# Softmax weights in PSUM, the mask on ScalarE, and two matmuls a bank in the last half chunk

## The chip, the cores and the metric

The kernel runs on one core of a Trainium2 chip. The metric is the device time of one execution in microseconds (us), the median of three runs: 639.03 us (638.97 to 640.16). Five engines work side by side, each with a queue of its own: TensorE (PE; its weight loads are listed as PEld), VectorE (DVE), ScalarE (ACT), GpSimd (POOL) and SyncE (SP), which here only issues DMAs. SBUF is the working memory; PSUM takes the results of matmuls. A PSUM bank is [128, 512] float32, and the core has eight.

## The reference, cut to what matters

```
x = A_x                                   # [2048, 640]
g = sigmoid((x * gate_w).sum(-1))
# A: 32 heads of 20, each position looks at 8 positions, 2 apart, at or before it
logits = einsum("bhsd,bhswd->bhsw", q, kg) * 20 ** -0.5
logits = where(idx >= 0, logits, -1e9)
a = einsum("bhsw,bhswd->bhsd", softmax(logits), vg) @ wo
# B: dense, Mish, dense, with 1728 hidden units
b = mish(x @ w1 + b1) @ w2
out = g * a + (1 - g) * b
```

## The kernel before, in words

All matmuls are float32 split in two: a high half, rounded to float32r, and a low half, the rest. `mm3` makes one product of three matmuls: high x high, high x low, low x high. For every operand ScalarE makes the high half (L337) and VectorE or GpSimd the low half (L340), into a `pair` tile. An operand thus costs one DMA, one ScalarE and one VectorE or GpSimd instruction before TensorE can use it.

The work in order of TensorE's stream: eight units of q, k, v (four groups of eight heads, two halves P of the positions), interleaved with the first layer (`mlp1`, 13 chunks of 128 hidden units by four blocks of 512 positions); then the second layer (`mlp2`); then the projection by wo (`wo_out`), whose VectorE sums (L954) form the output.

The second layer computes a 2 x 2 block product with seven products instead of eight, named a to g in `PRODUCTS`. Each has seven chunks of 128 hidden units (kc = 0 to 6). Its activations ("11", "21", "22", "t1" to "t4") lie in DRAM, written by `mish` with SP's DMAs and with GpSimd's adding DMAs (L613); its weights are w2 or sums of w2 (`s_d`, made by L704). 1728 = 13 x 128 + 64, so the last chunk of the second half of the hidden units has only 64 rows (FR); it meets kc = 6 of the products b, g and f. There the kernel before pads: the tiles keep 128 rows, the weights' lower 64 rows are zeros, the activations' lower rows are copies of finite data.

The attention runs on VectorE (`attention`), in two halves a unit: `scores` multiplies q by a window of k (L424) and sums over the head (L427) into `lg`; GpSimd adds -BIG/scale to the logits of partition 0 that look before the start (`bounded`, L435); VectorE takes the maximum (L442) and subtracts it (L443); ScalarE exponentiates (L444); `shares` divides by the sum, times the gate, and writes the weights `pw` (L452); `outputs` multiplies a window of v by `pw` (L458) and adds over the window (L463, L464, L466).

The order of every queue is written out by `Plan`: it walks through the tasks with a duration for each and hands out, engine by engine, what is ready, by rank. Low halves and a few sums may go to VectorE or GpSimd ("ANY"). While attention lasts, GpSimd may start such work only within a quiet time, and its instruction is then made to wait for the VectorE instruction ahead of that time (`follow`); quiet is, before, the sum L427 alone. Rings limit what is in flight: 8 banks, 21 pairs, 7 raw buffers.

Of the kernel before, what the change touches and what calls it, by code (L numbers as in the profile page):

```python
# [8 lines left out]
F32 = mybir.dt.float32  # L9
# [49 lines left out]
class Plan:  # L59
# [34 lines left out]
    def run(self):  # L94
# [34 lines left out]
        while left:  # L129
            again = not events or events[0][0] > now  # L130
            while again:
                again = False
                for e in self.LAG:
                    if busy[e]:
                        continue
                    fit = [t for t in ready[e] if fits(t)]
                    on = begun and loud
                    if e == "POOL":
                        fit += [t for t in shared if fits(t)]
                        if on:  # L140
                            fit = [t for t in fit if now + t.ns[0] <= quiet + 150 or t.rank < 0]
                    elif e == "DVE":
                        fit += [t for t in shared if fits(t) and (not on or due(t))]
                    if not fit:
                        continue
                    t = min(fit, key=lambda t: t.key)
                    if t.both:
                        shared.remove(t)
                        t.eng = e
                    else:  # L150
                        ready[e].remove(t)
                    if type(t.ns) is tuple:
                        t.ns = t.ns[e == "DVE"]
                    for b in t.take:
                        b.ring.free -= 1
                        b.ring.at += 1
                        b.t = b.make()
                    t.start = now
                    ins = t.fn(e) if t.both else t.fn()
                    if e == "POOL" and on and quiet > now and gate and ins:  # L160
                        self.follow(ins, gate)
                    if e == "DVE":
                        if t.kind:
                            begun = True
                            loud -= 1
                        if t.kind == "qk sum":
                            quiet, gate = now + t.ns, last
                        last = ins or last
                    if e == "PE":
                        begun_pe = max(begun_pe, t.pos)  # L170
                    busy[e] = again = True
                    end = over = now + t.ns * self.CARE.get(e, 1.0)
                    heapq.heappush(events, (over, n, "idle", e))
                    if t.land:
                        wire = max(wire, end) + t.land
                        end = wire + (0 if e == "SP" else self.ADDING)
# [36 lines left out]
def kernel(ctx: ExitStack, tc: tile.TileContext, x, wq, wo, w1, b1, w2, xt, gw, out):  # L213
# [3 lines left out]

    keep = ctx.enter_context(tc.tile_pool(name="keep", bufs=1))
    dram = ctx.enter_context(tc.tile_pool(name="dram", bufs=1, space=DRAM))
    psum = ctx.enter_context(tc.tile_pool(name="psum", bufs=8, space=PSUM))  # L220
    pe = ctx.enter_context(tc.tile_pool(name="pe", bufs=1, side="right"))
    at = ctx.enter_context(tc.tile_pool(name="at", bufs=1))

# [5 lines left out]
    plan = Plan({"bank": 8, "pair": NPAIR, "w": NW, "raw": NRAW, "raw1": 1, "hb": NH,  # L229
                 "ot": 1, "b": 11}, follow)  # L230

    def ps_buf():
        return plan.buf("bank", lambda: psum.tile([128, 512], F32, name="bank"))

    def pair_buf():
        return plan.buf("pair", lambda: pe.tile([128, 2, 512], F32R, name="pair", bufs=NPAIR))
# [31 lines left out]
    def mm_ns(n):  # L268
        return 13.5 + (n + 15) // 16 * 16 / 2.4
# [7 lines left out]

    A.preload_act_table_set("mish")
    bias = keep.tile([128, FC + 1], F32)
    bound = keep.tile([1, 7, 7], F32)  # L280
    zt = keep.tile([128, 2, 8], F32)
    gate = keep.tile([128, 2, 8], F32)
    gc = keep.tile([128, 2, 8], F32)
# [120 lines left out]
    def attention(u, P, hq, ready, gates):  # L404
# [27 lines left out]

        def bounded(a, b, after):
            b = min(b, 7)
            return add("POOL", 3400, lambda: G.tensor_tensor(lg[0:1, a:b, :, 0:7], lg[0:1, a:b, :, 0:7],  # L435
                       bound[:, a:b, None, :].to_broadcast([1, b - a, HQ, 7]), op=OP.add), [cg] + after, rank=-1)

        def softmax(a, rank, after):

# [176 lines left out]
    def mish(src, n, fc, tb, after, hold, late=0, home=None):  # L616
# [15 lines left out]
        def at(name):  # L632
            return name, P, kc

        def rest(name, of, after):

            return [put(at(name), of, after, rows=high)] if n < 128 else []

        if (half, h) == (0, 0):
            done[at("11")] = [put(at("11"), here, [a], [hb])]  # L640
            done[at("t1")] = [put(at("t1"), here, [a], [hb])]
        elif (half, h) == (0, 1):
            done[at("t3")] = [put(at("t3"), here, [a], [hb])]
            done[at("t1")] = [plus(at("t1"), here, [a] + done[at("t1")], [hb])]
        elif (half, h) == (1, 0):
            done[at("21")] = [put(at("21"), here, [a], [hb], low)]
            if n < 128:
                done[at("21")].append(dma(lambda: blk[at("21")][n:], here, [a], rank=0.5, hold=[hb], size=n * 2048))
            done[at("t4")] = [put(at("t4"), here, [a], [hb], low)] + rest("t4", lambda: blk[at("t1")][high], done[at("t1")])
        else:  # L650
            done[at("22")] = [put(at("22"), here, [a], [hb], low)]
            if n < 128:
                done[at("22")].append(dma(lambda: blk[at("22")][n:], here, [a], rank=0.5, hold=[hb], size=n * 2048))
            t2 = [put(at("t2"), here, [a], [hb], low)] + rest("t2", lambda: blk[at("t1")][high], done[at("t1")])
# [34 lines left out]
    def sums_of_w2(kc):  # L689
# [24 lines left out]
        s4 = sum_of((o2, 256), (o1, 256), (a2, 0), OP.subtract, [s3])  # L714
        m = add("ACT", act_ns(128), lambda: A.activation(apart.t[:, 256:384], apart.t[:, :128], AF.Copy, scale=-1.0), d[2:], rank=LATER, hold=[apart], late=2500)
        q = sum_of((apart, 384), (apart, 0), (apart, 128), OP.add, [m, s4], n=128)
        if kc == KH - 1:
            s4 = add("POOL", 300, lambda: G.memset(o2.t[FR:, 256:], 0.0), [s4], rank=-1.0, hold=[o2])
            q = add("POOL", 300, lambda: G.memset(apart.t[FR:, 384:], 0.0), [q], rank=-1.0, hold=[apart])
        done["s", kc] = [kept(0, 512, o1, 0, [s2]), kept(512, 256, o2, 0, [s3]), kept(896, 256, o2, 256, [s4]),  # L720
                         kept(768, 128, apart, 256, [m]), kept(1152, 128, apart, 384, [q])]

    def load_minus(src, n):

        raw, p = stage(True), pair_buf()
        d = dma(lambda: raw.t[:, :n], src, take=[raw], size=n * 512)
        a = add("ACT", act_ns(n), lambda: A.activation(p.t[:, 0, :n], raw.t[:, :n], AF.Copy, scale=-1.0), [d], rank=SOON, take=[p], hold=[raw])
        b = add("DVE", dve_ns(n), lambda: V.scalar_tensor_tensor(p.t[:, 1, :n], raw.t[:, :n], -1.0, p.t[:, 0, :n].bitcast(F32),
                op0=OP.mult, op1=OP.subtract), [a], rank=SOON, hold=[raw, p])
        p.ready = [a, b]  # L730
        return p

# [18 lines left out]
    def load_step(i):  # L751
        k, kc = steps[i]
        name, of, _ = PRODUCTS[k]
        at = 0
        if name == "a":
            p = load_pair(lambda: w2[kc][:, :384], "ANY", n=384, wide=i > 2)
        elif name == "b":
# [30 lines left out]
    def mlp2(mid):  # L788
# [72 lines left out]
        for i, (k, kc) in enumerate(steps):  # L861
# [17 lines left out]
            for part in parts:  # L879
# [7 lines left out]
                for c in kcs:  # L887
# [4 lines left out]
                    def run(part=part, keys=keys, p=p, at=at, acts=acts, first=first, stop=stop, names=names, name=name):  # L892
# [5 lines left out]
                    last = add("PE", 9 * len(part) / 3 * mm_ns(512), run,  # L898
                               [last] + p.ready + sum((acts[P].ready for P in Ps), []) + [read[key] for key in keys if key in read and c == 0],
                               take=take if c == kc else [], hold=[bank[key] for key in keys] + [p] + [acts[P] for P in Ps])  # L900
                    if c == KH - 1:
# [171 lines left out]
```

## Time and profile before

| what | value |
|---|---|
| median of three runs | 639.03 us |
| profiled execution: span, first to last instruction | 636.9 us (its time with start and end is not listed; the median lies 2.1 us above the span) |
| TensorE busy | 631.9 us, 99%, 2805 matmuls, granted clock 1.00 throughout |
| VectorE busy | 584.1 us, 92% |
| ScalarE, GpSimd busy | 277.4 us (44%), 215.2 us (34%) |
| a matmul with 512 columns | 386 ns long |
| chain that ended last | TensorE 99% |

How to read it: a row of a group names the line, engine, operation and tiles (out<-in), shapes, count, then busy us and the mean ns of one, then idle time in front of them. A timeline row has start, length, engine, line. Matmuls overlap, so the distance between two starts, not the length, is what one costs in a stream. An idle engine that nobody waits for costs nothing.

### The profile page before, as it was taken

How to read it: one execution, taken by the hardware profiler on the slowest of the kernel's cores; microseconds unless marked ns; L12 is line 12 of the kernel's file. 1: busy time of each engine (PE TensorE's matmuls, PEld its weight loads, DVE VectorE, ACT ScalarE, POOL GpSimd, SP SyncE). 2: the span in 40 equal slices, each digit the busy share in tenths (PEclk: the TensorE clock that was granted, in tenths of full speed). 3: DMA queues.
4: the chain of work that ended last, by engine and by line, in shares of the span. 5: the costliest groups of instructions: out<-in, count | busy, mean ns of one | idle time of the engine just before them, and what ended most of it. 6: DMA issues, size and time to landing. Idle time of an engine off the chain costs nothing.

```text
span 636.9 us, 8494 instructions
## 1 busy us (share of the span) xinstructions
PE 631.9 (99%) x2805; PEld 526.2 (83%) x2805; DVE 584.1 (92%) x584; ACT 277.4 (44%) x565; POOL 215.2 (34%) x157
## 2 busy tenths in 40 slices
PE   9999999999999999999999999999999999999997
PEld 6888888888888888888888888888888888888886
DVE  7888999999999999999899989799999999999941
ACT  7553353435436332542524244584676426721100
POOL 2212313131414442132343423204107328967310
PEclk9999999999999999999999999999999999999999
DMA  9999998867954994798499955989996758844642
GB/s 327 373 283 180 190 263 227 229 174 223 296 172 86 271 258 93 222 218 178 84 245 214 219 122 147 254 274 282 312 286 220 226 159 288 289 155 149 193 158 82
DMA packets 91323, 137.26 MB, mean 216 GB/s; under 512 B 12128, under 2 KB 41184, under 8 KB 91216
## 3 DMA queue, kind: packets, MB, share of 16 engines
q1 hardware_dynamic: 83600, 122.83, 62.6%
q0 software_dynamic: 7680, 13.90, 14.8%
q8 instruction: 22, 0.36, 0.2%
q14 instruction: 21, 0.17, 0.1%
HBM read 77.11 MB, written 57.81 MB: 212 GB/s over the span
## 4 chain that ended last, share of the span: by engine, by line
PE 99%; DVE 0%; issue 0%
PE bank L374 33%; PE bank L372 33%; PE bank L373 33%; PE bank L510 1%; PE bank L319 1%; DVE kvq L954 0%; DVE lg L315 0%
## 5 line engine op out<-in xcount | busy, mean ns | idle before, releaser
L372 PE MATMUL bank<-pair 128*128 128x512 f32 (+1 forms) x476 | 183.8, 386 | 0.0
L374 PE MATMUL bank<-pair 128*128 128x512 f32 (+1 forms) x476 | 183.7, 386 | 0.0
L373 PE MATMUL bank<-pair 128*128 128x512 f32 (+1 forms) x476 | 183.7, 386 | 0.0
L373 PEld LDWEIGHTS bank<-pair 128*128 128x128 f32 x476 | 89.3, 188 | 17.2
L374 PEld LDWEIGHTS bank<-pair 128*128 128x128 f32 x476 | 89.4, 188 | 17.1
L372 PEld LDWEIGHTS bank<-pair 128*128 128x128 f32 x476 | 89.3, 188 | 17.0
L424 DVE TENSOR_TENSOR pr<-kvq 128x2560 f32<-128x2560 f32 x32 | 90.8, 2839 | 3.5 <-DMA kvq<-kvq 1.6
L337 ACT ACTIVATE pair<-raw 128x512 fp32r<-128x512 f32 (+3 forms) x122 | 72.0, 615 | 48.4 <-DMA raw<-o 21.5
L458 DVE TENSOR_TENSOR pr<-kvq,pw 128x2560 f32<-128x2560 f32 x32 | 91.1, 2848 | 0.9
L427 DVE TENSOR_REDUCE lg<-pr 128x128 f32<-128x2560 f32 x32 | 90.2, 2818 | 0.6
L516 ACT ACTIVATE kvq<-bank 128x320 f32<-128x320 f32 x64 | 28.3, 442 | 114.7 <-PE bank L374 114.7
L435 POOL TENSOR_TENSOR lg<-lg,bound 1x168 f32<-1x168 f32 (+1 forms) x16 | 68.8, 4303 | 20.4 <-DVE lg L427 18.7
L625 ACT ACTIVATE hb<-bank,bias 128x512 f32<-128x512 f32 x52 | 35.9, 690 | 90.7 <-PE bank L374 77.2
L374 PE MATMUL bank<-pair,kvq 128*128 128x512 f32 (+1 forms) x188 | 72.6, 386 | 0.0
L372 PE MATMUL bank<-pair,kvq 128*128 128x512 f32 (+1 forms) x188 | 72.6, 386 | 0.0
L373 PE MATMUL bank<-pair,kvq 128*128 128x512 f32 (+1 forms) x188 | 72.6, 386 | 0.0
L340 POOL TENSOR_TENSOR pair<-raw,pair 128x496 fp32r<-128x496 f32 (+2 forms) x31 | 42.6, 1386 | 86.4 <-ACT pair L337 30.0
L372 PE MATMUL bank<-pair,w 128*128 128x512 f32 x182 | 70.8, 389 | 0.0
L373 PE MATMUL bank<-pair,w 128*128 128x512 f32 x182 | 70.8, 389 | 0.0
L374 PE MATMUL bank<-pair,w 128*128 128x512 f32 x182 | 70.8, 389 | 0.0
L340 DVE TENSOR_TENSOR pair<-raw,pair 128x512 fp32r<-128x512 f32 (+1 forms) x91 | 63.9, 721 | 5.2 <-ACT pair L337 5.2
L337 ACT ACTIVATE pair<-hb 128x512 fp32r<-128x512 f32 (+3 forms) x63 | 38.8, 615 | 42.7 <-DMA hb<-o 16.0
(89 smaller groups left out, 873.9 us busy)
## 6 DMA issues: line engine op xcount, KB each, us to landing
actt<-hb SPq DMA_DIRECT2D x52, 256.0 KB, 4.6
act<-hb SPq DMA_DIRECT2D x38, 256.0 KB, 4.6
raw<-actt SPq DMA_DIRECT2D x32, 256.0 KB, 4.5
raw<-act SPq DMA_DIRECT2D x29, 256.0 KB, 4.0
actt<-hb POOLq DMA_DIRECT2D x26, 256.0 KB, 6.2
actt<-actt POOLq DMA_DIRECT2D x24, 256.0 KB, 5.4
hb<-actt SPq DMA_DIRECT2D x24, 256.0 KB, 4.5
kvq<-in_xt SPq DMA_DIRECT2D x16, 320.0 KB, 7.2
```

The source lines that it names most:

```text
L319: nc.tensor.matmul(warm_bank.t, idle[:, :128], idle, start=True, stop=True)
L337: a = add("ACT", act_ns(n), lambda: A.activation(hi(), raw(), AF.Copy), after, rank=rank, take=take, hold=hold)
L340: return (V if e == "DVE" else G).tensor_tensor(lo(), raw(), hi().bitcast(F32), op=OP.subtract)
L372: nc.tensor.matmul(ps, ah, bh, start=first, stop=False, skip_group_check=more)
L373: nc.tensor.matmul(ps, ah, bl, start=False, stop=False, skip_group_check=more)
L374: nc.tensor.matmul(ps, al, bh, start=False, stop=last, skip_group_check=more)
L424: return V.tensor_tensor(pr, window(kv, s0, 0), q[:, s0:s0 + 2, None, :].to_broadcast([128, 2, W, QF]), op=OP.mult)
L427: V.tensor_reduce(lg_w[:, s0:s0 + 2], pr.rearrange("p s w (h d) -> p s w h d", d=DH), op=OP.add, axis=AX.X)
L435: return add("POOL", 3400, lambda: G.tensor_tensor(lg[0:1, a:b, :, 0:7], lg[0:1, a:b, :, 0:7], bound[:, a:b, None, :].to_broadcast([1, b - ...
L458: V.tensor_tensor(pr.rearrange("p s w (h d) -> p s w h d", d=DH), vw, pw[:, s0:s0 + 2, :, :, None].to_broadcast([128, 2, W, HQ, DH]), op=O ...
L516: a = add("ACT", 330, lambda: A.activation(kv[:, 7 + s], ps.t[:, QF:3 * QF].rearrange("p (a b) -> p a b", a=2), AF.Copy), [done] + before, ...
L625: a = add("ACT", 595, lambda: A.activation(to(it()), src(), AF.Mish, bias=bias[:n, fc:fc + 1]), after + [bias_in], rank=NEXT, take=[] if h ...
```

## The change

Three things change, and the planner's order follows.

The softmax weights `pw` move from SBUF to PSUM, into the eighth bank; matmuls keep seven. VectorE writes them there (L452) and reads them in L458, and the planner now counts that product, too, as a quiet time for GpSimd.

-BIG is no longer added by GpSimd. `bound` is filled with -BIG/scale, and ScalarE copies it over the logits, one small instruction for each of the seven positions concerned, 56 in all.

In the last chunk of b, g and f the 64 rows are loaded twice, into partitions 0 to 63 and 64 to 127. The weights' operand holds the high half above and the low half below, the activations' operand the high half in both; one matmul of 128 rows makes high x high + low x high, and one of 64 rows makes high x low. The padding DMAs and fills go.

```
-                        if t.kind == "qk sum":
+                        if t.kind in ("qk sum", "pv"):
                             quiet, gate = now + t.ns, last
...
-    psum = ctx.enter_context(tc.tile_pool(name="psum", bufs=8, space=PSUM))
+    NBANK = 7
+    psum = ctx.enter_context(tc.tile_pool(name="psum", bufs=1, space=PSUM))
...
-    pw = at.tile([128, 8, W, HQ], F32, name="pw")
+    pw = psum.tile([128, 8, W, HQ], F32, name="pw")
...
-        G.memset(bound, 0.0)
-        G.affine_select(bound, bound, pattern=[[1, 7], [1, 7]], compare_op=OP.is_ge,
-                        fill=-BIG / scale, base=-7, channel_multiplier=0)
+        G.memset(bound, -BIG / scale)
...
         def bounded(a, b, after):
             b = min(b, 7)
-            return add("POOL", 3400, lambda: G.tensor_tensor(lg[0:1, a:b, :, 0:7], lg[0:1, a:b, :, 0:7],
-                       bound[:, a:b, None, :].to_broadcast([1, b - a, HQ, 7]), op=OP.add), [cg] + after, rank=-1)
+            def run():
+                for s in range(a, b):
+                    A.activation(lg[0:1, s, :, 0:7 - s], bound[:, :, 0:7 - s], AF.Copy)
+            return add("ACT", 220 * (b - a), run, [cg] + after, rank=-1)
...
-        if kc == KH - 1:
-            s4 = add("POOL", 300, lambda: G.memset(o2.t[FR:, 256:], 0.0), [s4], rank=-1.0, hold=[o2])
-            q = add("POOL", 300, lambda: G.memset(apart.t[FR:, 384:], 0.0), [q], rank=-1.0, hold=[apart])
...
+    def twice(raw, src, n, after=()):
+        def both():
+            for a in (0, FR):
+                nc.sync.dma_start(raw.t[a:a + FR, :n], src())
+        return [add("SP", 900, both, after, take=[raw], size=n * 512)]
+    def load_low_w(src, n, sign, after=()):
+        raw, p = stage(True), pair_buf()
+        d = twice(raw, src, n, after)
+        a = add("ACT", act_ns(n), lambda: A.activation(p.t[:, 0, :n], raw.t[:, :n], AF.Copy, scale=sign), d, rank=SOON, take=[p], hold=[raw])
+        b = add("DVE", dve_ns(n), lambda: V.scalar_tensor_tensor(p.t[FR:, 0, :n], raw.t[FR:, :n], sign, p.t[FR:, 0, :n].bitcast(F32),
+                op0=OP.mult, op1=OP.subtract), [a], rank=SOON, hold=[raw, p])
...
+    def load_low_act(src, after):
+        raw, p = stage(True), pair_buf()
+        d = twice(raw, src, 512, after)
+        a = add("ACT", act_ns(512), lambda: A.activation(p.t[:, 0], raw.t, AF.Copy), d, rank=SOON, take=[p], hold=[raw])
+        def low(e):
+            return (V if e == "DVE" else G).tensor_tensor(p.t[:FR, 1], raw.t[:FR], p.t[:FR, 0].bitcast(F32), op=OP.subtract)
...
+        if kc == KH - 1 and name in "bgf":
...
+            loaded[i] = p, 0, [load_low_act(lambda P=P: blk[of, P, kc][:FR], done[of, P, kc]) for P in range(2)]
...
+                            if low:
+                                more = (key[0] + name) in ("pb", "qb", "wg", "vf")
+                                nc.tensor.matmul(bank[key].t, p.t[:, 0, c:c + 128], acts[P].t[:, 0], start=False, stop=False, skip_group_check=more)
+                                nc.tensor.matmul(bank[key].t, p.t[:FR, 0, c:c + 128], acts[P].t[:FR, 1], start=False, stop=True, skip_group_check=more)
+                                continue
```

How the order moves, at three places. First TensorE, at the end of product b, where the last two chunks are taken bank by bank (the pairs named are activations, weights). Before:

```order
L372 MATMUL bank_3413<-pair_3751,pair_3746 128x512
L373 MATMUL bank_3413<-pair_3751,pair_3746 128x512
L374 MATMUL bank_3413<-pair_3751,pair_3746 128x512
L372 MATMUL bank_3413<-pair_3811,pair_3761 128x512
L373 MATMUL bank_3413<-pair_3811,pair_3761 128x512
L374 MATMUL bank_3413<-pair_3811,pair_3761 128x512
L372 MATMUL bank_3429<-pair_3751,pair_3746 128x512
```

and after:

```order
L371 MATMUL bank_3446<-pair_3795,pair_3778 128x512
L372 MATMUL bank_3446<-pair_3795,pair_3778 128x512
L373 MATMUL bank_3446<-pair_3795,pair_3778 128x512
L929 MATMUL bank_3446<-pair_3826,pair_3809 128x512
L930 MATMUL bank_3446<-pair_3826,pair_3809 128x512
L371 MATMUL bank_3463<-pair_3795,pair_3778 128x512
```

Three matmuls of the last chunk have become two, L929 with 128 rows and L930 with 64; the rest of TensorE's order is as it was.

Second ScalarE, at the first -BIG of the program (hb is a first-layer result, read from its bank with Mish; kvq1 takes k, v and q of unit 1). Before:

```order
L625 ACTIVATE hb_733<-bank_685,bias_70 128x512
L628 ACTIVATE hb_733<-hb_733 128x512
L337 ACTIVATE w_737<-raw1_673 128x640
L625 ACTIVATE hb_779<-bank_716,bias_70 128x512
L715 ACTIVATE raw_708<-raw_708 128x128
L516 ACTIVATE kvq1_213<-bank_762 128x320
```

and after:

```order
L628 ACTIVATE hb_730<-bank_682,bias_70 128x512
L631 ACTIVATE hb_730<-hb_730 128x512
L336 ACTIVATE w_734<-raw1_670 128x640
L437 ACTIVATE lg_215<-bound_71 1x8x3
L437 ACTIVATE lg_215<-bound_71 1x8x2
L437 ACTIVATE lg_215<-bound_71 1x8
L628 ACTIVATE hb_778<-bank_713,bias_70 128x512
L712 ACTIVATE raw_705<-raw_705 128x128
L519 ACTIVATE kvq1_213<-bank_761 128x320
```

Three copies that wait for VectorE's sum now stand ahead of evictions of banks.

Third VectorE, late in product d, up to the low half (hb_4733 before, hb_4761 after) that TensorE uses in the same step of the product. Before:

```order
L458 TENSOR_TENSOR pr_217<-kvq2_3212,pw_216 128x2560
L340 TENSOR_TENSOR kvq0_4452<-raw1_4670,kvq0_4452 128x640
L340 TENSOR_TENSOR pair_4740<-raw_4668,pair_4740 128x384
L340 TENSOR_TENSOR pair_4742<-hb_4659,pair_4742 128x512
L340 TENSOR_TENSOR pair_4758<-raw_4685,pair_4758 128x512
L340 TENSOR_TENSOR pair_4763<-raw_4694,pair_4763 128x384
L340 TENSOR_TENSOR pair_4774<-hb_4733,pair_4774 128x512
L340 TENSOR_TENSOR pair_4786<-raw_4700,pair_4786 128x512
L463 TENSOR_TENSOR pr_217<-pr_217 128x2x640
```

and after:

```order
L469 TENSOR_TENSOR kvq2_3235<-pr_217 128x320
L339 TENSOR_TENSOR pair_4822<-hb_4761,pair_4822 128x512
L339 TENSOR_TENSOR pair_4827<-raw_4755,pair_4827 128x512
L379 STREAM_TRANSPOSE ot_4842<-kvq2_3235 128x4x5x32
L445 TENSOR_REDUCE mx_218<-lg_215 128x32
```

The sums that follow L458 (the L463, L464 and L466 of before) now stand ahead of that low half, where they stood behind it, and the 640-column half of wo ahead of it has gone to GpSimd.

More of the change, by code (lines that the diff above doesn't have):

```diff
@@ L227, in follow @@
                           mybir.DependencyInfo(mybir.DependencyClass.Sync, mybir.DependencyReason.DATA), reason="beside")
-    plan = Plan({"bank": 8, "pair": NPAIR, "w": NW, "raw": NRAW, "raw1": 1, "hb": NH,
+    plan = Plan({"bank": NBANK, "pair": NPAIR, "w": NW, "raw": NRAW, "raw1": 1, "hb": NH,
                  "ot": 1, "b": 11}, follow)
     def ps_buf():
-        return plan.buf("bank", lambda: psum.tile([128, 512], F32, name="bank"))
+        return plan.buf("bank", lambda: psum.tile([128, 512], F32, name="bank", bufs=NBANK))
     def pair_buf():
@@ L279 @@
     bias = keep.tile([128, FC + 1], F32)
-    bound = keep.tile([1, 7, 7], F32)
+    bound = keep.tile([1, HQ, 7], F32)
     zt = keep.tile([128, 2, 8], F32)
@@ L633, in at @@
             return name, P, kc
-        def rest(name, of, after):
-            return [put(at(name), of, after, rows=high)] if n < 128 else []
         if (half, h) == (0, 0):
@@ L646, in mish @@
             done[at("21")] = [put(at("21"), here, [a], [hb], low)]
-            if n < 128:
-                done[at("21")].append(dma(lambda: blk[at("21")][n:], here, [a], rank=0.5, hold=[hb], size=n * 2048))
-            done[at("t4")] = [put(at("t4"), here, [a], [hb], low)] + rest("t4", lambda: blk[at("t1")][high], done[at("t1")])
+            done[at("t4")] = [put(at("t4"), here, [a], [hb], low)]
         else:
             done[at("22")] = [put(at("22"), here, [a], [hb], low)]
+            t2 = [put(at("t2"), here, [a], [hb], low)]
             if n < 128:
-                done[at("22")].append(dma(lambda: blk[at("22")][n:], here, [a], rank=0.5, hold=[hb], size=n * 2048))
-            t2 = [put(at("t2"), here, [a], [hb], low)] + rest("t2", lambda: blk[at("t1")][high], done[at("t1")])
+                t2.append(put(at("t2"), lambda: blk[at("t1")][high], done[at("t1")], rows=high))
             done[at("t3")] = [plus(at("t3"), here, [a] + done[at("t3")], [hb], n)]
@@ L729, in load_minus @@
                 op0=OP.mult, op1=OP.subtract), [a], rank=SOON, hold=[raw, p])
+        p.ready = [a, b]
+        return p
+    def twice(raw, src, n, after=()):
[9 more added lines that the diff above has]
+                op0=OP.mult, op1=OP.subtract), [a], rank=SOON, hold=[raw, p])
+        p.ready = [a, b]
+        return p
+    def load_low_act(src, after):
[4 more added lines that the diff above has]
+            return (V if e == "DVE" else G).tensor_tensor(p.t[:FR, 1], raw.t[:FR], p.t[:FR, 0].bitcast(F32), op=OP.subtract)
+        b = add("ANY", either("ANY", 512), low, [a], rank=SOON, hold=[p, raw])
         p.ready = [a, b]
@@ L754, in load_step @@
         at = 0
+        if kc == KH - 1 and name in "bgf":
+            if name == "b":
+                p = load_low_w(lambda: w2[KH + kc][:FR, :384], 384, -1.0)
+            elif name == "g":
+                p = load_low_w(lambda: s_d[kc][:FR, 896:1280], 384, 1.0, done["s", kc])
+            else:
+                p = load_low_w(lambda: w2[KH + kc][:FR, 384:], 256, 1.0)
+            loaded[i] = p, 0, [load_low_act(lambda P=P: blk[of, P, kc][:FR], done[of, P, kc]) for P in range(2)]
+            return
         if name == "a":
@@ L890, in mlp2, with run @@
                     stop = {key: c == KH - 1 for key in keys}
-                    def run(part=part, keys=keys, p=p, at=at, acts=acts, first=first, stop=stop, names=names, name=name):
+                    def run(part=part, keys=keys, p=p, at=at, acts=acts, first=first, stop=stop, names=names, name=name,
+                            low=c == KH - 1 and name in "bgf"):
                         for (P, x), key in zip(part, keys):
                             c = at + names.index(x) * 128
+                            if low:
[3 more added lines that the diff above has]
+                                continue
                             mm3(bank[key].t, tuple(p.t[:, j, c:c + 128] for j in range(2)), tuple(acts[P].t[:, j] for j in range(2)),
                                 first[key], stop[key], (key[0] + name) in ("pb", "qb", "wg", "rd", "vf"))
-                    last = add("PE", 9 * len(part) / 3 * mm_ns(512), run,
+                    last = add("PE", (2 if c == KH - 1 and name in "bgf" else 3) * len(part) * mm_ns(512), run,
                                [last] + p.ready + sum((acts[P].ready for P in Ps), []) + [read[key] for key in keys if key in read and c == 0],
```

## The prediction

> **What bounds the kernel now.** I read the page's head first, then TensorE's waits, then the timeline at two places, and the groups of the engines last.
>
> ```profile
> span 636.9 us, 8494 instructions
> PE 631.9 (99%) x2805; PEld 526.2 (83%) x2805; DVE 584.1 (92%) x584; ACT 277.4 (44%) x565; POOL 215.2 (34%) x157
> PEclk9999999999999999999999999999999999999999
> ```
>
> TensorE is busy in 99% of the span at full clock. A busy PE alone proves little, because matmuls overlap; so the waits (engine and tile, releaser, total us, times, longest) and the pace:
>
> ```profile
> PE bank L319 <- DVE lg L315: 1.2, 1, 1.2
> PEld bank L510 <- ACT pair L337: 0.5, 1, 0.5
> ```
>
> Both belong to the first 5 us. After that no matmul and no weight load is listed as waiting. The timeline near the end (start, length):
>
> ```profile
> 622.09 0.39 PE L372 MATMUL bank<-pair,kvq 128*128 128x512 f32 x1
> 622.32 0.39 PE L373 MATMUL bank<-pair,kvq 128*128 128x512 f32 x1
> ...
> 632.74 0.39 PE L374 MATMUL bank<-pair,kvq 128*128 128x512 f32 x1
> 633.17 0.69 DVE L954 TENSOR_TENSOR kvq<-bank,kvq 128x512 f32<-128x512 f32 x1 [2.71 <-PE bank L374]
> ```
>
> From 622.09 to 632.74 there are 48 matmuls, so 47 steps: 0.2266 us from start to start. Each lasts 0.39, so two are always in flight. The time of the kernel is therefore a count of matmuls: 1.2 us before the first, the stream, and about 4 us of eviction and store behind it. VectorE is the engine that can break this:
>
> ```profile
> core 0: us, PE busy (x) PEld busy (x) DVE busy (x) ACT busy (x) POOL busy (x), PEclk, DMA share, GB/s
> 520.00:560.00 40.00, 40.00 (x179) 33.10 (x178) 39.97 (x54) 25.18 (x45) 29.51 (x4) 1.00 0.88 294
> 560.00:600.00 40.00, 40.00 (x178) 33.14 (x177) 39.76 (x38) 7.61 (x13) 28.01 (x15) 1.00 0.46 145
> ```
>
> It has 0.03 and 0.24 us idle in these two stretches of 40, so what it delivers to TensorE can only come sooner if it has less to do.
>
> **The matmuls.** In products b, g and f the last chunk takes two matmuls a bank instead of three. Banks: 6 + 6 + 4 = 16, so 16 matmuls go, at 0.2266 each: **3.63 us**. All of it lies on the path. The 16 that follow a 128-row matmul now contract 64 rows; the program has no such matmul before, so their price needs bounds. From above:
>
> ```profile
> L372 PE MATMUL bank<-pair 128*128 128x512 f32 (+1 forms) x476 | 183.8, 386 | 0.0
> L372 PEld LDWEIGHTS bank<-pair 128*128 128x128 f32 x476 | 89.3, 188 | 17.0
> ```
>
> If the array had to run empty at each change between 128 and 64 rows, a step would grow from 227 to 386 ns, 159 more, and with the weight load exposed too to 574, 347 more. There are two changes for each of the 16, so 32: +5.1 or +11.1 us. From below, a matmul of half the rows can hardly be shorter, since the step goes by the columns:
>
> ```profile
> 10.53 0.38 PE L372 MATMUL bank<-pair,kvq 128*128 128x496 f32 x1
> 10.75 0.39 PE L373 MATMUL bank<-pair,kvq 128*128 128x496 f32 x1
> ```
>
> 0.22 for 496 columns, 0.2266 for 512; at the very most all 16 would vanish, another 3.6. I take 0, because these rows are the nearest: in them the step is set by columns alone, through every change of weights. [...]
>
> **Softmax weights in PSUM.** 32 products (L458) now read one operand from PSUM and 16 (L452) write it. VectorE's nearest rows, both sides SBUF and one side a bank:
>
> ```profile
> L458 DVE TENSOR_TENSOR pr<-kvq,pw 128x2560 f32<-128x2560 f32 x32 | 91.1, 2848 | 0.9
> L954 DVE TENSOR_TENSOR kvq<-bank,kvq 128x512 f32<-128x512 f32 x10 | 6.7, 682 | 9.4 <-PE bank L374 9.4
> L808 DVE TENSOR_TENSOR kvq<-kvq 128x512 f32<-128x512 f32 x4 | 2.6, 677 | 0.0
> L452 DVE TENSOR_TENSOR pw<-lg,sm 128x256 f32<-128x256 f32 x16 | 11.6, 723 | 0.5
> ```
>
> 682 against 677: 5 ns for a PSUM source, 0.2 us over 32. No row writes PSUM from VectorE; I bound it at plus or minus 0.1 us, 1.6 us over 16, and take 0. All of it is VectorE's, not the path's. [...]
>
> A product with one SBUF operand also lets GpSimd work beside it, which the planner now does (it counts "pv" as a quiet time):
>
> ```profile
> 561.84 1.76 POOL L340 TENSOR_TENSOR pair<-hb,pair 128x512 fp32r<-128x512 f32 x1
> 562.35 0.67 DVE L808 TENSOR_TENSOR kvq<-kvq,bank 128x512 f32<-128x512 f32 x1
> 569.59 3.65 DVE L458 TENSOR_TENSOR pr<-kvq,pw 128x2560 f32<-128x2560 f32 x1
> 570.52 6.37 POOL L821 TENSOR_TENSOR kvq<-kvq,w 128x512 f32<-128x512 f32 x2
> ```
>
> Beside GpSimd the instruction with a bank keeps its 0.67 and L458, both operands in SBUF, stretches to 3.65. So I expect L458 at 2.8 everywhere.
>
> **What VectorE sheds.** Counted in the orders, its 512-column low halves go from 123 to 108 plus 5 of 64 partitions: 10 fewer.
>
> ```profile
> 536.78 0.68 DVE L340 TENSOR_TENSOR pair<-hb,pair 128x512 fp32r<-128x512 f32 x1
> 537.38 0.68 DVE L340 TENSOR_TENSOR pair<-raw,pair 128x512 fp32r<-128x512 f32 x1
> 538.68 0.39 PE L373 MATMUL bank<-pair 128*128 128x512 f32 x1
> ```
>
> They step by 0.60, so 6 us. The first of these rows is the scarcest in the second layer's main part: it ends at 537.46 and TensorE uses it at 538.68, 1.2 us of slack. In the new order TensorE gets there 12 matmuls (2.7 us) sooner. Ahead of that place VectorE has nine 512-column halves fewer (91 to 79, plus 3 of 64 partitions), 5.4 us; the rest of the difference about cancels (two 640-column halves, one of 496, five small sums fewer; one more of each output sum L463, L464, L466). Slack: 1.2 - 2.7 + 5.4, about 4 us. Without the relief it is -1.5.
>
> **The -BIG writes.** GpSimd loses its 16 adds, ScalarE gets 56 tiny copies:
>
> ```profile
> L435 POOL TENSOR_TENSOR lg<-lg,bound 1x224 f32<-1x224 f32 x8 | 42.9, 5358 | 19.1 <-DVE lg L427 17.6 <-PE bank L374 1.6
> L435 POOL TENSOR_TENSOR lg<-lg,bound 1x168 f32<-1x168 f32 x8 | 26.0, 3248 | 1.2 <-DVE lg L427 1.1
> L520 ACT ACTIVATE hx<-bank 128x16 f32<-128x16 f32 x64 | 12.7, 198 | 0.0
> L625 ACT ACT_TABLE_LOAD x13 | 16.7, 1283 | 1.0 <-PE bank L374 0.7
> ACT L444 <- DVE lg L443: 3.3, 3, 1.8
> POOL lg L435 <- DVE lg L427: 18.7, 9, 13.3
> ```
>
> GpSimd is freed of 69 us, which pays for its extra low halves. ScalarE adds 56 x 0.2 = 11 us and drops two table loads, 2.6: net 8.5 on an engine 44% busy, hidden. The new wait counts for more: the copies stand in ScalarE's queue behind VectorE's reduce, and behind them stand evictions of banks. By the exponentials, which stand there already, ScalarE waits about 3 us in all; by GpSimd's adds up to 13.3 at a time. I take the exponentials, since the planner places both by readiness.
>
> **Seven banks.** The tightest place, if nothing else moved:
>
> ```profile
> 590.29 0.68 DVE L954 TENSOR_TENSOR hb<-bank,hb 128x512 f32<-128x512 f32 x1
> 592.17 0.39 PE L372 MATMUL bank<-pair,kvq 128*128 128x512 f32 x1
> ```
>
> The matmul at 592.17 opens a bank, and the seventh bank back is read until 590.97: 1.2 us to spare even with seven. TensorE will come 3.6 us sooner, so VectorE must read 2.4 us sooner. It can: counted as above, nine 512-column halves and five 512-column sums or gate products fewer stand ahead of the last low halves, 14 x 0.60 = 8.4 us. If it could not, 2.4 of the 3.6 would be lost.
>
> **DMAs.** 570 issues on SP instead of 567: nine loads become two of half the rows each, two padding copies and four fills go. GpSimd's queue keeps 56. Nothing waits there for TensorE, so 0.
>
> **Sum.** -3.63 on a span of 636.9 gives 633.3. The median of 639.03 lies 2.1 above that span (start and end outside it), which stays: **635.4 us**.
>
> **Rivals.**
> 1. The array runs empty at each change of rows: 32 x 0.159 = 5.1, so 640.5, slower by 0.2%; with the weight load exposed 32 x 0.347 = 11.1, so 646.5. The change turns from gain to loss at 3.63 / 32 = 0.113 us for one change. For it: matmuls of this trace overlap by 159 ns, so there is something to lose, and no row has 64 rows. Against it: every step of the trace is set by columns alone. [...]
> 2. VectorE becomes the wait, the relief being eaten by GpSimd work that runs past a quiet window and stretches the next sum. Place: the low half at 538.68. Lost 1.5, so 636.9.
> 3. Seven banks, at 592.17: lost 2.4, so 637.8, hardly to be told from no change. ScalarE held 13 us by one reduce would act in the same way, through late evictions.
> 4. It does not do what it says: the 64-row matmuls cost as much as the two they replace, because each change costs about the break-even 0.113: 639.
>
> **Chances.** As summed, 635.4: 0.50. Rival 2: 0.11. Rival 3: 0.06, half of it on either side of the bound. Rival 4 and other near-nothing: 0.05. Rival 1: 0.28, two thirds of it near 640.5, the rest above. What a measurement of this kernel can tell from no change is about 0.2%, 1.3 us (637.7 to 640.3). Faster: 0.50 + 0.11 + 0.03 = 0.64; same: 0.08; slower: 0.28. Range: below, 634.5, allowing 1 us for a shorter 64-row matmul or tail; above, 641.0, which takes in the drained case and leaves out its exposed weight load. The likeliest case's own range is 634.5 to 636.5.
>
> **What will show it.** Right: 2789 matmuls; the step over the end of b, g and f stays 0.227 through the 64-row matmuls; no wait of PE in the list; L458 near 2.82; VectorE less busy from 520 to 600 than its 99%. Wrong: steps of 0.39 or more at the lines of the two-matmul chunk (rival 1); a PE wait on VectorE's low halves after 450 us (2); a PE wait on a bank, read by VectorE near 590 or by ScalarE behind a -BIG copy (3).

## The result, and the profile after

| what | before | after |
|---|---|---|
| median | 639.03 us (638.97 to 640.16, 5 runs) | 642.20 us (641.59 to 642.34, 5 runs) |
| ratio to before, 95% interval | | 1.0043 (1.0031 to 1.0054) |
| span of the profiled execution | 636.9 us | 640.4 us |

The changed kernel is 0.43% slower. It was forecast to be 0.6% faster, and 642.2 lies above the range given. The head of its page and its chain:

```profile
span 640.4 us, 8510 instructions
PE 634.9 (99%) x2789; PEld 521.7 (81%) x2789; DVE 566.5 (88%) x566; ACT 281.0 (44%) x619; POOL 163.6 (26%) x156
PE 99%; DMA 1%; DVE 0%; ACT 0%; SPq 0%; issue 0%
```

The sixteen matmuls are gone (2789 against 2805), VectorE is busy 17.6 us less, and yet TensorE is busy 3.0 us longer. No engine or transfer holds it up. What is new stands in the list of waits, on the weight loads (engine, tile and line, releaser, total us, times, longest):

```profile
PEld bank L930 <- issue: 5.3, 15, 0.4
PEld bank L371 <- issue: 3.7, 15, 0.2
PE bank L320 <- DVE lg L316: 1.2, 1, 1.2
PE bank L513 <- ACT pair L336: 0.3, 1, 0.3
```

The last two lines belong to the first 6 us, as before. The first two name no releaser ("issue" is time in which the engine waited for nothing that the profile shows): L930 is the 64-row matmul, and L371 the 128-row matmul that comes next (the sixteenth of each is listed under another releaser). The timeline of TensorE at the end of product b shows both (start, length):

```profile
443.51 0.39 PE L373 MATMUL bank<-pair 128*128 128x512 f32 x1
443.74 0.39 PE L929 MATMUL bank<-pair 128*128 128x512 f32 x1
444.05 0.50 PE L930 MATMUL bank<-pair 64*128 64x512 f32 x1
444.48 0.50 PE L371 MATMUL bank<-pair 128*128 128x512 f32 x1
444.81 0.39 PE L372 MATMUL bank<-pair 128*128 128x512 f32 x1
445.04 0.39 PE L373 MATMUL bank<-pair 128*128 128x512 f32 x1
```

From start to start the steps are 0.23, 0.31, 0.43, 0.33, 0.23 us. The step into the 64-row matmul, the step out of it and the one after that exceed 0.2266 by 0.09, 0.20 and 0.11: **0.40 us for one 64-row matmul, 0.20 for each change between 128 and 64 rows**. The weight loads at the same place:

```profile
443.51 0.19 PEld L929 LDWEIGHTS bank<-pair 128*128 128x128 f32 x1
444.05 0.18 PEld L930 LDWEIGHTS bank<-pair 64*128 64x128 f32 x1 [0.35 <-issue]
444.48 0.19 PEld L371 LDWEIGHTS bank<-pair 128*128 128x128 f32 x1 [0.25 <-issue]
444.59 0.19 PEld L372 LDWEIGHTS bank<-pair 128*128 128x128 f32 x1
```

Where the rows stay at 128, the weights of L372 load at 444.59, 0.22 us before their matmul starts at 444.81. At a change (L930, L371) the load begins only when its matmul is listed as starting.

The whole accounts for itself. From the start of the 60th matmul to the start of the last one took 616.41 us before and 619.18 after, 2.77 more. In that stretch the steps of after exceed 0.227 by 6.38 us in all, all of it around the sixteen; 6.38 - 3.63 = 2.75. The other 0.7 us by which the spans differ are 0.5 ahead of that stretch (the first matmuls of q waited for a load of their weights' operand) and 0.2 behind it. The medians differ by 3.2 us, a little less than the spans, since after's time outside the span is 1.8 us (642.21 less 640.4 in the profiled run) where 2.1 was taken.

### The profile page after: what moved, and what is told of

It is laid out like the page before. It is cut to its first block, busy times and chain, and to the rows that moved or that the text cites. A ratio compares the mean times of both kernels' runs of the same rounds, so it can differ in the third digit from the quotient of the medians.

```text
span 640.4 us, 8510 instructions
## 1 busy us (share of the span) xinstructions
PE 634.9 (99%) x2789; PEld 521.7 (81%) x2789; DVE 566.5 (88%) x566; ACT 281.0 (44%) x619; POOL 163.6 (26%) x156
## 4 chain that ended last, share of the span: by engine, by line
PE 99%; DMA 1%; DVE 0%; ACT 0%; SPq 0%; issue 0%
PE bank L371 32%; PE bank L373 32%; PE bank L372 32%; PE bank L930 1%; PE bank L513 1%; DMA hb<-in_wq 1%; PE bank L929 1%; DVE kvq L991 0%; ACT pair L336 0%; SPq L345 0%
## 5 line engine op out<-in xcount | busy, mean ns | idle before, releaser
L371 PE MATMUL bank<-pair 128*128 128x512 f32 (+1 forms) x460 | 179.1, 389 | 0.0
L372 PE MATMUL bank<-pair 128*128 128x512 f32 (+1 forms) x460 | 177.5, 386 | 0.0
L373 PE MATMUL bank<-pair 128*128 128x512 f32 (+1 forms) x460 | 177.5, 386 | 0.0
L371 PEld LDWEIGHTS bank<-pair 128*128 128x128 f32 x460 | 86.3, 188 | 19.5 <-issue 3.4
L373 PEld LDWEIGHTS bank<-pair 128*128 128x128 f32 x460 | 86.4, 188 | 16.5
L372 PEld LDWEIGHTS bank<-pair 128*128 128x128 f32 x460 | 86.4, 188 | 16.0
L423 DVE TENSOR_TENSOR pr<-kvq 128x2560 f32<-128x2560 f32 x32 | 90.3, 2822 | 8.2 <-ACT kvq L519 6.2
L461 DVE TENSOR_TENSOR pr<-kvq,pw 128x2560 f32<-128x2560 f32 x32 | 90.2, 2820 | 1.0
L336 ACT ACTIVATE pair<-raw 128x512 fp32r<-128x512 f32 (+2 forms) x117 | 69.0, 616 | 48.5 <-DVE kvq L852 9.3
L339 POOL TENSOR_TENSOR pair<-raw,pair 128x512 fp32r<-128x512 f32 (+2 forms) x36 | 48.0, 1351 | 140.5 <-ACT pair L336 52.7
L371 PE MATMUL bank<-pair,kvq 128*128 128x512 f32 (+1 forms) x188 | 72.7, 387 | 0.0
L372 PE MATMUL bank<-pair,kvq 128*128 128x512 f32 (+1 forms) x188 | 72.6, 386 | 0.0
L371 PE MATMUL bank<-pair,w 128*128 128x512 f32 x182 | 70.8, 389 | 0.0
L372 PE MATMUL bank<-pair,w 128*128 128x512 f32 x182 | 70.8, 389 | 0.0
L339 DVE TENSOR_TENSOR pair<-raw,pair 128x512 fp32r<-128x512 f32 (+2 forms) x81 | 57.7, 731 | 4.9 <-ACT pair L336 4.8
L466 DVE TENSOR_TENSOR pr<-pr 128x1280 f32<-128x1280 f32 x32 | 50.5, 1577 | 0.9
L336 ACT ACTIVATE pair<-hb 128x512 fp32r<-128x512 f32 (+3 forms) x60 | 36.9, 614 | 29.2 <-DMA hb<-actt 11.8
```

Of the source, the lines that this page charges most:

```text
L336: a = add("ACT", act_ns(n), lambda: A.activation(hi(), raw(), AF.Copy), after, rank=rank, take=take, hold=hold)
L339: return (V if e == "DVE" else G).tensor_tensor(lo(), raw(), hi().bitcast(F32), op=OP.subtract)
L371: nc.tensor.matmul(ps, ah, bh, start=first, stop=False, skip_group_check=more)
L372: nc.tensor.matmul(ps, ah, bl, start=False, stop=False, skip_group_check=more)
L373: nc.tensor.matmul(ps, al, bh, start=False, stop=last, skip_group_check=more)
L423: return V.tensor_tensor(pr, window(kv, s0, 0), q[:, s0:s0 + 2, None, :].to_broadcast([128, 2, W, QF]), op=OP.mult)
```

## The experiments

Medians are in us, ratios are to before, with their 95% interval; the kernel before stood at 639.36 beside runs e1 to e4 and at 639.19 beside e5 to e8. "Beyond the pace" is the time by which TensorE's steps, from start to start in the timeline, exceed 0.227 us, summed from its 60th matmul on.

| run | changes 128/64 rows | median | ratio | beyond the pace |
|---|---|---|---|---|
| after | 32 | 642.20 | 1.0043 (1.0031 to 1.0054) | 6.38 |
| e1_rows128 | 0 | 635.16 | 0.9939 (0.9927 to 0.9951) | 0 |
| e2_chunk_alone | 0 | 638.64 | 0.9986 (0.9977 to 0.9995) | 2.02 |
| e3_old_chunk | 0 | 639.25 | 0.9999 (0.9990 to 1.0008) | 0 |
| e4_before_64 | 32 | 645.45 | 1.0100 (1.0087 to 1.0113) | 6.38 |
| e5_all_three_64 | 32 | 645.71 | 1.0098 (1.0085 to 1.0111) | 6.47 |
| e6_paired | 16 | 639.01 | 0.9996 (0.9987 to 1.0005) | 3.23 |
| e7_psum_weights | 0 | 635.28 | 0.9935 (0.9923 to 0.9947) | 0 |
| e8_mask_on_act | 0 | 635.71 | 0.9951 (0.9934 to 0.9968) | 0.85 |

The theory was that each change of rows costs TensorE 0.20 us. The rivals were that the rest of the change (seven banks, -BIG on ScalarE, the new order of VectorE) costs it, and that it is each 64-row matmul that costs, not the change.

**The second matmul on 128 rows.** The pairs hold the high half of the activations twice anyway, so the low half can be made on all 128 partitions, and the second matmul then contracts 128 rows:

```
-            return (V if e == "DVE" else G).tensor_tensor(p.t[:FR, 1], raw.t[:FR], p.t[:FR, 0].bitcast(F32), op=OP.subtract)
+            return (V if e == "DVE" else G).tensor_tensor(p.t[:, 1], raw.t, p.t[:, 0].bitcast(F32), op=OP.subtract)
...
-                                nc.tensor.matmul(bank[key].t, p.t[:FR, 0, c:c + 128], acts[P].t[:FR, 1], start=False, stop=True, skip_group_check=more)
+                                nc.tensor.matmul(bank[key].t, p.t[:, 0, c:c + 128], acts[P].t[:, 1], start=False, stop=True, skip_group_check=more)
```

> The changed kernel, but the second matmul of the last chunk contracts 128 rows as the first does: the activations' low half is made on all 128 partitions, so it also adds low x low. 16 matmuls fewer than before, no matmul of 64 rows. Theory R (a change between 128 and 64 rows costs about 0.40 us for each pair of changes, 6.4 us in all): every step stays 0.227, 635.4 us, that is 3.6 below before and 6.4 or more below the changed kernel. Theory P (the loss comes from the other two parts: seven banks, weights in PSUM, copies on ScalarE): about 642, as the changed kernel.

Measured: 635.16 us. Its head, and its timeline at the same place:

```profile
span 634.1 us, 8512 instructions
PE 628.3 (99%) x2789; PEld 523.1 (83%) x2789; DVE 567.0 (89%) x566; ACT 281.9 (44%) x619; POOL 163.0 (26%) x156
```

```profile
443.76 0.39 PE L929 MATMUL bank<-pair 128*128 128x512 f32 x1
443.99 0.39 PE L930 MATMUL bank<-pair 128*128 128x512 f32 x1
444.21 0.39 PE L371 MATMUL bank<-pair 128*128 128x512 f32 x1
444.44 0.39 PE L372 MATMUL bank<-pair 128*128 128x512 f32 x1
```

Every step is 0.22 to 0.23 again. The stretch from the 60th to the last matmul is 612.77 us, 3.64 below before: sixteen matmuls at 0.2266, with nothing given back. The engines' loads are those of after within 0.9 us, apart from TensorE. So all that after loses against e1 hangs on the rows of one matmul in each of sixteen banks.

**The other parts with the old chunk.** Before, with `pw` in PSUM, seven banks, "pv" as a quiet time and -BIG on ScalarE; the padded three-matmul chunk stays. Beside before:

```
+                        if t.kind in ("qk sum", "pv"):
...
+    NBANK = 7
...
+    pw = psum.tile([128, 8, W, HQ], F32, name="pw")
...
+                    A.activation(lg[0:1, s, :, 0:7 - s], bound[:, :, 0:7 - s], AF.Copy)
```

> The changed kernel with the last chunk as before: three matmuls of 128 rows; weights in PSUM, seven banks and copies on ScalarE stay. Theory R: 639.0, as before, with VectorE less busy. Theory P: 642 or up to 645.8, three matmuls on top of the loss.

Measured: 639.25 us, ratio 0.9999. The stretch is 616.39 us against 616.41, and no matmul waits behind the start. Seven banks instead of eight, ScalarE's copies and the new order cost TensorE nothing that can be measured, and gain nothing as long as TensorE is the only bound.

**64 rows put into the kernel before.** Its third matmul (low x high) of the last chunk reads only the 64 rows that aren't padding; nothing else changes:

```
+                            if low:
+                                for n, i, j in ((128, 0, 0), (128, 0, 1), (64, 1, 0)):
+                                    nc.tensor.matmul(bank[key].t, p.t[:n, i, c:c + 128], acts[P].t[:n, j], start=False, stop=i == 1,
...
```

> Before, unchanged but for one thing: the third matmul of the last chunk in b, g and f contracts only the upper 64 rows (the weights' lower rows are zeros). As many matmuls as before, 16 of 64 rows, each between matmuls of 128. Theory R: 639.0 + 6.4 = 645.4. Theory P: 639.0.

Measured: 645.45 us, 1.0% slower; beyond the pace 6.38 us, the same as in after to the second decimal. Behind the start the same two kinds of wait appear (the sixteenth at L372 is listed under ScalarE):

```profile
PEld bank L898 <- issue: 5.6, 16, 0.4
PEld bank L372 <- issue: 3.7, 15, 0.2
```

With e1 and e3 this shows the cause: the rows alone bring the loss, without the rest of the change, and taking them away removes it.

**By change or by matmul.** Two kernels hold the one and vary the other. In e5 all three matmuls of that chunk contract 64 rows: three times as many 64-row matmuls, but still two changes a bank.

```
+                                for n, i, j in ((64, 0, 0), (64, 0, 1), (64, 1, 0)):
```

> Before, with all three matmuls of the last chunk in b, g and f on 64 rows (the lower rows of the weights are zeros): 48 matmuls of 64 rows in 16 runs of three, as many changes of rows (32) as with one. If the price belongs to the change: as with one such matmul, 645.4. If it belongs to each matmul of 64 rows: three times 6.4 on 639.0, 658.

Measured: 645.71 us, beyond the pace 6.47. Its timeline (the three 64-row matmuls share a row):

```profile
443.49 0.39 PE L374 MATMUL bank<-pair 128*128 128x512 f32 x1
443.81 0.96 PE L898 MATMUL bank<-pair 64*128 64x512 f32 x3
444.70 0.50 PE L372 MATMUL bank<-pair 128*128 128x512 f32 x1
445.04 0.40 PE L373 MATMUL bank<-pair 128*128 128x512 f32 x1
```

From 443.49 to 445.04 there are five steps, 1.55 us where 1.13 would be the pace: 0.42 by these rounded starts, 0.40 by the sum (6.47 us over sixteen banks), for two changes, with three 64-row matmuls between them as with one.

In e6, after's kernel is reversed in every second bank, so that the 64-row matmul of one bank stands next to that of the following bank: the same sixteen 64-row matmuls, but 16 changes.

```
+                turned = len(kcs) > 1 and kcs[-1] == KH - 1 and name in "bgf" and nth % 2
+                turn = kcs[::-1] if turned else kcs
...
+                                for n, j in ((FR, 1), (128, 0)) if turned else ((128, 0), (FR, 1)):
```

> The changed kernel with every second bank of the last chunk taken the other way round (its 64-row matmul first, then the 128-row one, then the chunk before), so that the 16 matmuls of 64 rows stand in 8 pairs and the changes of rows fall from 32 to 16. By the change: 642.2 - 3.2 = 639.0. By the matmul: 642.2.

Measured: 639.01 us, beyond the pace 3.23, half of after's 6.38:

```profile
443.55 0.39 PE L373 MATMUL bank<-pair 128*128 128x512 f32 x1
443.78 1.48 PE L932 MATMUL bank<-pair 128*128 128x512 f32 x4
445.09 0.40 PE L371 MATMUL bank<-pair 128*128 128x512 f32 x1
445.32 0.39 PE L372 MATMUL bank<-pair 128*128 128x512 f32 x1
```

The row with x4 holds the last chunk of two banks, 128, 64, 64 and 128 rows (the row names the shape of its first). Its four steps take 1.31 us where 0.91 would be the pace: 0.40, once for two banks. The price is by change: two 64-row matmuls side by side lost the 0.40 that one lost in after.

**The two-matmul chunk alone.** Now that the chunk was worth 3.6 us, were the other parts needed to collect it? e2 is e1's chunk in the kernel before: eight banks, `pw` in SBUF, "pv" no quiet time, -BIG on GpSimd. Beside e1:

```
-    pw = psum.tile([128, 8, W, HQ], F32, name="pw")
+    pw = at.tile([128, 8, W, HQ], F32, name="pw")
...
-                    A.activation(lg[0:1, s, :, 0:7 - s], bound[:, :, 0:7 - s], AF.Copy)
+            return add("POOL", 3400, lambda: G.tensor_tensor(lg[0:1, a:b, :, 0:7], lg[0:1, a:b, :, 0:7],
...
```

> Before, with the two-matmul chunk alone, both matmuls on 128 rows (low x low added); eight banks, weights in SBUF, -BIG on GpSimd. If the relief of VectorE is not needed: 635.4. If it is (the prediction's slack of 1.2 us at a place that TensorE reaches 2.7 us sooner): a wait of TensorE on a VectorE low half late in product d, 636.9 or more.

Measured: 638.64 us (636.80 to 639.42), ratio 0.9986. Most of the gain is lost. The waits of the profiled run, which took 637.93:

```profile
PE bank L373 <- DVE pair L340: 1.5, 2, 0.7
PEld bank L373 <- DVE pair L340: 2.3, 2, 1.2
```

The place is in the projection by wo, and this is VectorE, then TensorE, then ScalarE and GpSimd there:

```profile
575.42 2.83 DVE L458 TENSOR_TENSOR pr<-kvq,pw 128x2560 f32<-128x2560 f32 x1
578.16 0.68 DVE L988 TENSOR_TENSOR kvq<-bank,kvq 128x512 f32<-128x512 f32 x1
578.76 1.18 DVE L340 TENSOR_TENSOR pair<-raw,pair 128x512 fp32r<-128x512 f32 x1
...
578.87 0.39 PE L372 MATMUL bank<-pair,kvq 128*128 128x512 f32 x1
580.00 0.50 PE L373 MATMUL bank<-pair,kvq 128*128 128x512 f32 x1 [0.74 <-DVE pair L340]
...
576.48 0.64 ACT L337 ACTIVATE pair<-raw 128x512 fp32r<-128x512 f32 x1 [7.68 <-DMA raw<-o]
577.19 2.20 POOL L340 TENSOR_TENSOR pair<-raw,pair 128x512 fp32r<-128x512 f32 x1 [6.99 <-ACT pair L337]
```

The operand arrives late, since its rows of the attention's output (o) come late from DRAM; then its low half stands behind an attention product and a bank's eviction on VectorE, and at last takes 1.18 us instead of 0.68, beside a low half that GpSimd makes until 579.39. The next bank repeats it. VectorE has no idle time there to catch up:

```profile
560.00:600.00 40.00, 38.52 (x169) 31.24 (x169) 39.69 (x50) 8.36 (x14) 17.99 (x10) 1.00 0.53 166
```

(columns: stretch, length, then busy us and count of PE, PEld, DVE, ACT, POOL; clock, DMA share, GB/s). The profiled run loses 2.0 us of 3.6; the median of the timed runs loses 0.7 more, and no profile of such a run shows where. Four of the six longest of these runs list a granted clock of 0.996 or 0.997, where the profiled one has 0.999; the other two list 0.999 and 1.000, so the clock alone does not account for it.

**Which part brings the relief.** e7 is e2 with `pw` in PSUM, seven banks and "pv" quiet, with -BIG left on GpSimd. e8 is e2 with -BIG on ScalarE, with `pw` left in SBUF, eight banks and "pv" not quiet.

```
e7, beside e2
+                        if t.kind in ("qk sum", "pv"):
...
+    NBANK = 7
...
+    pw = psum.tile([128, 8, W, HQ], F32, name="pw")
```

```
e8, beside e2
+                    A.activation(lg[0:1, s, :, 0:7 - s], bound[:, :, 0:7 - s], AF.Copy)
```

> The two-matmul chunk on 128 rows with the softmax weights in PSUM (seven banks, GpSimd beside L458), -BIG still added by GpSimd. If the relief of VectorE comes from the quiet time beside L458: 635.2, no wait of TensorE. If it comes from taking -BIG off GpSimd: 638.6, as the chunk alone.

> The two-matmul chunk on 128 rows with -BIG copied by ScalarE, softmax weights still in SBUF, eight banks. If the relief of VectorE comes from taking -BIG off GpSimd: 635.2. If it comes from the quiet time beside L458: 638.6, with TensorE waiting for low halves near 580 as in the chunk alone.

Measured: 635.28 us for e7, 635.71 (635.13 to 639.71) for e8. Heads of e2, e7 and e8, in this order:

```profile
PE 629.4 (99%) x2789; PEld 523.9 (82%) x2789; DVE 585.6 (92%) x590; ACT 276.1 (43%) x565; POOL 190.4 (30%) x149
```

```profile
PE 628.3 (99%) x2789; PEld 522.9 (83%) x2789; DVE 569.5 (90%) x566; ACT 275.1 (43%) x563; POOL 177.1 (28%) x173
```

```profile
PE 628.8 (99%) x2789; PEld 523.6 (82%) x2789; DVE 583.1 (92%) x590; ACT 284.0 (45%) x621; POOL 136.0 (21%) x132
```

e7's three edits together take 16.1 us off VectorE (585.6 to 569.5), and no matmul waits behind the start. Most of it is work that moves: 24 instructions fewer on VectorE, 24 more on GpSimd; 3.5 us are the writes of `pw` (last section). Whether "pv" as a quiet time would do the same with `pw` in SBUF was not tried. Late in the program VectorE stays as full in e7 as in e2, 39.86 us of 40 against 39.69:

```profile
560.00:600.00 40.00, 40.00 (x178) 33.14 (x177) 39.86 (x40) 9.46 (x15) 30.60 (x19) 1.00 0.61 204
```

So it is not idle time at that place that saves e7, but what VectorE had got done by then and in which order; that much is argued from the loads, not shown. -BIG on ScalarE takes 2.5 off VectorE and 54 off GpSimd; one wait at the place of e2 (580.19) remains, 0.85 us beyond the pace:

```profile
PE bank L371 <- DVE pair L338: 0.6, 1, 0.6
```

So "either the one or the other" was too narrow a question: the first is enough by itself, the second nearly, though it hardly relieves VectorE. Together (e1) they give nothing more than the first.

## Why the prediction was wrong

**The step that failed** is the price of the 64-row matmul: "I take 0, because these rows are the nearest: in them the step is set by columns alone, through every change of weights." Measured, each change of rows costs 0.20 us, 32 x 0.20 = 6.4 us, which turns -3.6 into +2.8. The rows quoted (496 against 512 columns) varied the columns and never the rows, so they had nothing to say on a change of rows. They decided it only because they were the nearest there were. An operation that the trace of before does not hold had a break-even of 0.113 us, between bounds of 0 and 0.347; that called for chances near even, not for 0.50 to 0.28.

**The bounds were right, the range was not.** 0.20 lies between the two prices estimated from the lengths in before (386 ns a matmul, 188 a weight load, 227 a step): 0.159 (the array runs empty) and 0.347 (the weight load exposed too). The range ended at 641.0, just above the lower of the two, and left out what lay between, so 642.2 fell outside. Rival 1 named the cost, one at each change of rows, and its place. Its sign, steps of 0.39 or more there, fits in part: the price of two changes is spread over three steps, 0.32, 0.43 and 0.33, and only one of them reaches 0.39. That no matmul is listed as waiting was to be a sign of being right, and it held all the same: the loss stands in the steps and in the rows of the weight loads.

It is the change that costs and not the number of 64-row matmuls behind it: 0.40 us for each bank with three of them in e5 (6.47 us over sixteen), 0.40 with one in after (6.38 over sixteen). Whether the array runs empty at a change, no run here shows. Rival 1's first sum, 5.1 us lost and 640.5, was too low, as it used the lower of the two estimates; 6.4 were lost, a net of +2.8.

**What held, by its own steps.**

- Sixteen matmuls at 0.2266, 3.63 us, all on the path: e1's stretch is 3.64 shorter, and e1's median of 635.16 stands 0.2 from the 635.4 forecast for the likeliest case. That closeness is in part luck: in e1's profiled run (635.84 us, span 634.1) the 60th matmul starts 0.5 us later than before, 0.3 us more lie behind the last start, and 1.7 us instead of 2.1 lie outside the span.
- Seven banks: no wait of TensorE on a bank, in after, e1, e3 or e7. DMAs at nothing: only the first operand's load moved the start by some tenths.
- -BIG hidden: ScalarE did wait more than the 3 us taken, but no matmul waited for it behind the start. The line of after's waits:

```profile
ACT lg L437 <- DVE lg L426: 14.0, 9, 3.2
```

- L458 at 2.8 everywhere:

```profile
L461 DVE TENSOR_TENSOR pr<-kvq,pw 128x2560 f32<-128x2560 f32 x32 | 90.2, 2820 | 1.0
```

  The mean is 2820 ns, 28 less than before, but 26 of the 28 belong to one product, the row of 3.65 us that the prediction shows. The other 31 took 2.78 to 2.83 us with both operands in SBUF, also beside GpSimd (2.83 at 138.07, last section), so that row was no sample of the rest. The 5 ns more for a read of PSUM do not show: 2820 ns on average, against 2822 for those 31.
- VectorE less busy from 520 to 600 us: 75.16 us of 80 in after, where it had been 79.73.

```profile
520.00:560.00 40.00, 40.00 (x177) 33.15 (x178) 36.60 (x50) 23.07 (x46) 5.13 (x4) 1.00 0.78 248
560.00:600.00 40.00, 40.00 (x171) 31.45 (x171) 38.56 (x40) 9.41 (x15) 25.34 (x15) 1.00 0.57 183
```

**What was off without deciding.** VectorE's relief was put at 6 us, from its 512-column halves alone; 17.6 came; by the lengths of the groups, those halves are 8.2 of it and the writes of `pw` 4.7. Rival 2, VectorE as the wait, is real as soon as the relief is missing (e2), but its place was wrong: not at 538.7 with a slack worked out as -1.5, but 40 us later, in the projection, where the attention's output comes late. The price of writing PSUM was bounded at 0.1 us either way; it is 0.22 us in favour (below).

**What stays open.** Why a change costs 0.20 and not 0.16 or 0.35. The trace shows that the weights for the new shape are not loaded ahead; whether the time is the array running empty, the load, or both, no run here separates. The ends of matmuls are modelled in the profile, so the 0.159 and 0.347 made from their lengths were rough to begin with. Nor was a change to other row counts than 64 tried.

## What to carry to other kernels

In a stream of matmuls that sets the time, keep the contracted rows the same: here a matmul of half the rows cost as much as one of all (48 of 64 rows in e5 took the steps 6.47 us beyond the pace, 16 in e4 6.38), and going there and back 0.40 us more, nearly two matmuls (measured for 64 against 128 rows, with 512 columns). Fill the rows with something harmless instead, as e1 does, which at 635.16 us (0.9939) is faster than both kernels; where short matmuls can't be avoided, put them next to each other (3.23 us beyond the pace in e6, 6.38 in after). And when the trace before holds no instance of an operation, ask what the nearest rows vary: if it isn't what the change varies, they give no price, and the chances belong on both sides of the break-even.

## What the runs showed that was not expected

VectorE wrote the same 128 x 256 product sooner into PSUM than into SBUF. From the groups of e2 (SBUF) and e7 (PSUM):

```profile
L452 DVE TENSOR_TENSOR pw<-lg,sm 128x256 f32<-128x256 f32 x16 | 10.5, 654 | 0.5
```

```profile
L453 DVE TENSOR_TENSOR pw<-lg,sm 128x256 f32<-128x256 f32 x16 | 6.9, 434 | 0.5
```

654 against 434 ns, 3.5 us over the sixteen. Whether it is the bank or the tile's layout in it was not tried.

GpSimd, too, fares differently beside the product that reads `pw`. Before, and then in e7:

```profile
138.07 2.83 DVE L458 TENSOR_TENSOR pr<-kvq,pw 128x2560 f32<-128x2560 f32 x1
138.11 3.29 POOL L435 TENSOR_TENSOR lg<-lg,bound 1x224 f32<-1x224 f32 x1 [0.82 <-DVE lg L427]
```

```profile
138.14 2.82 DVE L459 TENSOR_TENSOR pr<-kvq,pw 128x2560 f32<-128x2560 f32 x1
138.18 0.66 POOL L436 TENSOR_TENSOR lg<-lg,bound 1x224 f32<-1x224 f32 x1 [0.18 <-DVE lg L428]
```

The same add takes 3.29 us beside the product with both operands in SBUF, and ends behind it; beside the product with one operand in PSUM it takes 0.66. The product takes the same time in both. In this pair it is GpSimd that is held up; the prediction had taken VectorE to be the one that stretches. e7 changes the order as well, so it is not shown that the operand's place alone does this.

The other surprise is how little stood between a gain and none. The two-matmul chunk is worth 3.6 us only while the low halves of the projection come in time: in e2 it keeps about 0.9 of them, and either of two reliefs, 16 us on VectorE or 54 us on GpSimd, restores nearly all.
